# Even part of a fused DFT and feed-forward kernel leaves its bank mid-sum, mixed by unit over VectorE, ScalarE and GpSimd; late last tile; early edge products

## The chip, the cores and the metric

The kernel runs on one core of one Trainium2 chip. The metric is the device time of an execution in microseconds (us). One early execution of the kernel before took 1646 us. A difference under 2% is called "within 2%" in the prediction. Five engines matter: TensorE (PE in the profile; its weight loads are PEld), VectorE (DVE), ScalarE (ACT), GpSimd (POOL) and SyncE (SP), which only issues transfers here.

## The reference

```python
def _attn_ref(x):                       # x: (8, 3008, 256)
    X = np.fft.fft(x, axis=1)
    X = np.fft.fft(X, axis=2)
    return X.real.astype(np.float32)

def _moe_ref(x, w_in, w_out):           # 24064 tokens, 256 -> 2048 -> 256
    h = np.maximum(x @ w_in, 0.0)
    return (h * h @ w_out).astype(np.float32)

def reference(x, moe_w_in, moe_w_out):
    y = _attn_ref(x)
    return _moe_ref(y.reshape(-1, 256), moe_w_in, moe_w_out)
```

## The kernel before

The kernel uses the symmetry of the transform. Folded inputs go through one table product along the sequence and give P (even part) and Q (odd part). The transform along the 256 features is multiplied into the first weights once, at the start: G1 for P and G2 for Q. A token and its mirror then need `relu(E + O)` and `relu(E - O)`, with E = G1'P and O = G2'Q. One row of Q is an exception: it belongs to the even part (the "edge") and must keep its sign in the mirror.

The work is cut into 25 chunks of up to 512 such pairs, and each chunk into units: one unit is 128 of the 2048 hidden features for 512 pairs. An ordinary unit takes three matmuls in one bank of PSUM, the memory that takes up TensorE's sums. E + O is read by ScalarE, then -2 O is added with the third weights G3, and ScalarE reads E - O:

```python
    def x_front(c, u):                                   # [indices shortened]
        xb = psx.tile([P, 512], F32, name="xb", tag="x")
        for sn, G in ((0, G1), (1, G2)):
            mm(xb, G[:, fs], PQ[b][sn][...], sn == 0, sn == 1)
        act(r_s(c, u), xb, AF.Relu)
        return (c, u, xb, None)

    def x_back(cur):                                     # two steps later
        if xb is None: return
        mm(xb, G3[:, fs], PQ[b][1][...], False, True)
        relu_d(c, u, lambda o, i: act(o, xb[:, :, i], AF.Relu))
```

Some units are split: two matmuls into two banks, and the two sums are made outside. That saves a matmul and costs VectorE three operations:

```python
    def x_split(c, u):
        xs = [xo, xe]                                    # two banks
        mm(xo, G2, Q); mm(xe, G1, P)
        act(bs[0], xs[0], AF.Copy, bias=0.0, scale=1.0)
        def add():
            stt(out=bs[1], in0=ebc[c], scalar=gE2[:, u : u + 1], in1=bs[0], op0=ALU.mult, op1=ALU.subtract)
            sat(r_s(c, u), bs[0])                        # relu(xe + bs[0]), VectorE
            relu_d(c, u, lambda o, i: sat(o, bs[1]))     # relu(xe + bs[1]), VectorE

    YZ = [(0, 0)] * 3 + [(2, 0)] * 3 + [(5, 1)] * 9 + [(7, 1)] * 9 + [(0, 0)]   # splits, ScalarE squares per chunk
```

VectorE (in some cases ScalarE) squares the hidden values, and the second layer runs through each chunk while the next one is being made:

```python
        for grp in groups:
            ops += [one(grp, j, fc) for j in range(len(grp)) for fc in range(NFC)]
...
    for c in range(4):                                   # output weights: 32-bit load, VectorE casts them
        nc.gpsimd.dma_start(out=wot[c], in_=moe_w_out[...])
    def wcast(c):
        nc.vector.tensor_copy(wout16[:, cs, :], wot[c])
    spread([(lambda c=c: wcast(c)) for c in range(4)], 3, 7)
    LAG = 2
    SQ = 1                                               # units between a finished unit and its square
```

## Time and profile before

| Measured | Value |
|---|---|
| time, median of 3 (the 1646 us among them) | 631.49 us |
| span of the profiled execution | 628.5 us |
| matmuls | 4682 |
| TensorE / VectorE / ScalarE / GpSimd busy | 96 / 85 / 76 / 11% |

From the page of the kernel before, parts 1 and 2: busy time of each engine (us, share of the span, instructions), and the granted TensorE clock, in tenths, in 40 equal slices of the span.

```profile
PE 606.4 (96%) x4682; PEld 446.9 (71%) x4682; DVE 536.8 (85%) x827; ACT 479.3 (76%) x872; POOL 68.8 (11%) x97
...
PEclk9979999999999999999999999999999999999999
...
```

A busy TensorE need not be at its peak: it counts as busy for 606.4 us, while the ideal spacings below sum to 596.1. So spacing matters more. The chain of waits has dozens of pieces like this one (start, length, what and how many):

```profile
86.01 0.88 PE po L73 x8
```

Eight second-layer matmuls of 256 columns start some 109 ns apart. In this trace the median spacing of each width N from 62 to 512 columns lies within 1.5 ns of N/2.4 + 2.5 ns (256 columns: 109 ns, 512: 217). I call that line the ideal spacing of a matmul of N columns, and whatever the next matmul starts later than that a gap. The 46 pieces of 31 columns lie above the line: they take 28 ns, and are counted at about 27. All ideal spacings sum to 596.1 us, all gaps to 17.3 us; the rest is 10.9 us ahead of the first matmul and 4.0 us after the last.

Where the gaps are is seen in the busy time by stretch (kernel before; stretch, its length, busy time and instructions of PE, PEld, DVE, ACT, POOL, granted clock, DMA share, GB/s):

```profile
24.00:40.00 16.00, 10.80 (x79) 7.33 (x78) 13.71 (x28) 15.30 (x33) 0.00 (x0) 1.00 0.91 190
40.00:48.00 8.00, 6.87 (x36) 4.46 (x35) 4.65 (x11) 2.69 (x6) 0.00 (x0) 0.57 0.04 0
...
450.00:500.00 50.00, 50.00 (x410) 39.26 (x408) 46.61 (x63) 39.43 (x70) 1.08 (x2) 1.00 0.31 49
```

In the first two stretches TensorE is not full, and in the second the clock falls to a mean of 0.57: the trace has it at one half from 40.2 us on for 6.8 us, and second-layer matmuls of 256 columns then start 213 ns apart in place of 109. I call this a half-clock spell. Later (third line) TensorE is full, beside a VectorE at 93% and a ScalarE at 79%. Two groups of waits of TensorE stand behind the start (the kernel before; total us, times, longest):

```profile
PE xb L73 <- ACT h L605: 4.1, 5, 1.8
PE pf L73 <- DVE cosT L279: 2.0, 2, 1.1
...
```

One small loss lies later. The edge products use weights of 3 columns (timeline of the kernel before; start, length, what):

```profile
142.95 0.60 PE L73 MATMUL po<-wout,h 128*128 128x256 f16 x4
143.48 0.64 PE L73 MATMUL pf<-cosT,eall 127*3 127x377 f16 x3
144.06 0.39 PE L73 MATMUL xb<-pt,G 128*128 128x512 f16 x1
```

Four matmuls should take 4 x 109 = 437 ns, yet the next starts 530 ns after the first: some 95 ns extra. The same comes on the way back, and also around the last tile's 16 columns: 18 times in all.

### The profile page before, as it was taken

Reading aid. Unit: us, or ns where it says so; the run is one execution under the profiler, and the core shown is the slowest. Engines: PE = TensorE matmul, PEld = TensorE weight load, DVE = VectorE, ACT = ScalarE, POOL = GpSimd, SP = SyncE. Lnnn points to the kernel's source line nnn. Section 1 sums busy time; section 2 is a strip of 40 time slices with the busy share of each in tenths; the row PEclk is TensorE's granted clock in tenths of the full one; section 3 lists DMA queues with packets and bytes.
Section 4 is the critical chain, followed back from the end, with each engine's and each line's share of the span. In section 5 each row is a group of like instructions: output and inputs, shape, how many; then the busy total and the mean of one; then the engine's idle time right before and its main releaser. Section 6 shows DMA issues by size and latency. Waiting matters only on the chain.

```text
span 628.5 us, 11983 instructions
## 1 busy us (share of the span) xinstructions
PE 606.4 (96%) x4682; PEld 446.9 (71%) x4682; DVE 536.8 (85%) x827; ACT 479.3 (76%) x872; POOL 68.8 (11%) x97
## 2 busy tenths in 40 slices
PE   3969999999999999999999999999999999999997
PEld 1547677776777777777777768777787778877786
DVE  8788799995988989889899879998999899999920
ACT  6768887777788788777887877877877778878871
POOL 8204043120120005000000000000000000000000
PEclk9979999999999999999999999999999999999999
DMA  8944477682591416714313314314233134131112
GB/s 282 300 83 138 120 181 205 156 225 57 91 208 36 59 44 170 138 34 59 43 51 44 57 34 63 43 47 48 54 56 43 51 43 59 52 46 48 52 52 68
DMA packets 37342, 57.21 MB, mean 91 GB/s; under 512 B 7262, under 2 KB 31490, under 8 KB 37286
## 3 DMA queue, kind: packets, MB, share of 16 engines
q0 software_dynamic: 7536, 30.21, 27.9%
q1 hardware_dynamic: 29702, 26.23, 13.4%
q8 instruction: 36, 0.59, 0.4%
q14 instruction: 20, 0.16, 0.1%
q10 hardware_dynamic: 48, 0.02, 0.0%
HBM read 29.02 MB, written 24.64 MB: 85 GB/s over the span
## 4 chain that ended last, share of the span: by engine, by line
PE 92%; DVE 6%; ACT 1%; issue 0%; DVEq 0%; POOL 0%; POOLq 0%; ACTq 0%
PE po L73 52%; PE xb L73 25%; PE pf L73 6%; PE xo L73 4%; PE xe L73 4%; DVE h L663 2%; PE warm L73 1%; DVE u L330 1%; DVE v L342 0%; DVE w L348 0%; DVE wout L723 0%; DVE tm L248 0%; ACT h L605 0%; DVE tm L236 0%; DVE tt L183 0%
## 5 line engine op out<-in xcount | busy, mean ns | idle before, releaser
L73 PE MATMUL po<-wout,h 128*128 128x256 f16 x3024 | 433.6, 273 | 0.0
L73 PEld LDWEIGHTS <-h 128*128 128x128 f16 x3024 | 287.2, 98 | 113.9 <-issue 0.4
L663 DVE TENSOR_TENSOR h<-h 128x2048 f16<-128x2048 f16 (+1 forms) x174 | 207.8, 1195 | 41.1 <-ACT h L651 36.5
L605 ACT ACTIVATE h<-xb 128x512 f16<-128x512 f32 (+1 forms) x270 | 159.2, 590 | 67.8 <-PE xb L73 67.1
L73 PE MATMUL xb<-qt,G 128*128 128x512 f16 (+11 forms) x720 | 203.6, 322 | 4.9 <-ACT h L605 4.1
L651 ACT ACTIVATE h<-xb 128x512 f16<-128x512 f32 (+2 forms) x286 | 160.4, 567 | 20.3 <-PE xb L73 13.9
L73 PEld LDWEIGHTS <-G 128*128 128x128 f16 x1384 | 130.3, 98 | 36.7 <-issue 9.6
L636 DVE CUSTOM_DVE_ANT_0 h<-xe,bs 128x512 f16<-128x512 f32 x228 | 145.9, 680 | 0.0
L73 PE MATMUL xb<-pt,G 128*128 128x512 f16 (+9 forms) x360 | 103.8, 324 | 0.3 <-DVE qt L424 0.2
L632 DVE SCALAR_TENSOR_TENSOR bs<-eb,gE,bs 128x512 f32<-128x512 f16 x114 | 85.0, 745 | 9.1 <-ACT bs L629 8.4
L629 ACT ACTIVATE bs<-xo 128x512 f32<-128x512 f32 x114 | 68.5, 601 | 21.0 <-PE xo L73 16.3
L557 ACT ACTIVATE os<-po 128x512 f32<-128x512 f32 x94 | 56.4, 600 | 19.1 <-PE po L73 16.7
L614 POOL DMA_DIRECT2D eb<-qt x28 | 15.4, 551 | 349.6 <-DVE bs L632 297.1
L73 PE MATMUL xo<-qt,G 128*128 128x512 f16 (+14 forms) x152 | 43.4, 327 | 0.0
L73 PE MATMUL xe<-pt,G 128*128 128x512 f16 (+14 forms) x152 | 43.4, 326 | 0.0
L330 DVE TENSOR_TENSOR u<-x 127x765 f16<-127x765 f32 x32 | 29.7, 945 | 0.0
L101 POOL DMA_INDIRECT x<-in_x_dram,idx x18 | 27.6, 1536 | 5.8 <-issue 4.5
L73 PEld LDWEIGHTS <-w 127*128 127x128 f16 (+1 forms) x192 | 21.6, 118 | 7.2 <-issue 1.4
L73 PE MATMUL pf<-cosT,w 127*128 127x377 f16 (+1 forms) x96 | 20.5, 327 | 2.0 <-DVE cosT L279 2.0
L124 POOL DMA_DIRECT2D x<-in_x_dram x14 | 7.9, 562 | 123.3 <-DVE u L334 122.7
L348 DVE TENSOR_TENSOR w<-v 127x381 f16<-127x381 f16 x64 | 20.7, 352 | 0.0
L73 PE MATMUL pf<-sinT,w 127*127 127x377 f16 (+1 forms) x96 | 20.7, 323 | 0.0
(103 smaller groups left out, 216.9 us busy)
## 6 DMA issues: line engine op xcount, KB each, us to landing
out_dram<-os SPq DMA_DIRECT2D x157, 128.0 KB
x<-in_x_dram POOLq DMA_DIRECT2D x14, 756.0 KB, 9.6
wst<-in_moe_w_in_dram POOLq DMA_DIRECT2D x4, 512.0 KB, 6.9
wot<-in_moe_w_out_dram POOLq DMA_DIRECT2D x4, 512.0 KB, 9.1
eb<-qt POOLq DMA_DIRECT2D x14, 128.0 KB, 6.7
x<-in_x_dram SPq DMA_DIRECT2D x2, 756.0 KB
x<-in_x_dram,idx POOLq DMA_INDIRECT x18, 10.7
gE<-G SPq DMA_DIRECT2D x16, 0.2 KB
```

The lines of the kernel that those rows point to most:

```text
L73: nc.tensor.matmul(o, l, r, start=start, stop=stop, skip_group_check=True)
L101: nc.gpsimd.indirect_dma_start(out=x4[0:NP, 2 + s, q : q + rows, :].rearrange("p q d -> p (q d)"), out_offset=None, in_=bass.AP(tensor=x.t ...
L330: return lambda: vt(u[k, s, q0 : q0 + NQ // 2, 1:D], x4[k, s, q0 : q0 + NQ // 2, 1:D], x4[k, 3 - s, ::-1, :][:, q0 : q0 + NQ // 2, D - 1 : ...
L348: return lambda: vt(w[k, i, q : q + 3, 0 : P - 1], vs[s][k, q : q + 3, 1:P], vs[s][k, q : q + 3, D - 1 : P : -1], op=ALU.add if i < 2 else ...
L557: act(os_, po, AF.Copy, bias=0.0, scale=HS * HS)
L605: act(r_s(c, u), xb, AF.Relu)
L614: nc.gpsimd.dma_start(out=ebc[c][:, o : o + l], in_=PQ[b][1][P - 1 : P, i : i + l].unsqueeze(1).to_broadcast([1, P, l]))
L629: act(bs[0], xs[0], AF.Copy, bias=0.0, scale=1.0)
L632: stt(out=bs[1], in0=ebc[c][:, 0:n], scalar=gE2[:, u : u + 1], in1=bs[0], op0=ALU.mult, op1=ALU.subtract)
L636: nc.vector._custom_dve(TENSOR_ADD_SAT, out=o, in0=xs[1], in1=t, s0=BIG, s1=0.0)
L651: relu_d(c, u, lambda o, i: act(o, xb[:, :, i], AF.Relu))
L663: vt(h2, h2, h2, op=ALU.mult)
```

## The change

The intent is to have fewer matmuls without filling VectorE. A taken unit has one bank and two matmuls. After E alone is in the bank, a copy of 2 E leaves it (VectorE in one operation, or ScalarE with an addition on GpSimd); then O is added in the bank, ScalarE reads relu(E + O), and VectorE reads the mirror as bank plus copy. The signs of G1 and G2 are turned so that this is a plain addition. X puts back the edge row's sign; it is made one step ahead. Which unit takes which way is a table. Other parts: the output weights are cast by their load (256 KB each in place of 512), two small operations go from VectorE to ScalarE, three warm-up matmuls (whose sums nobody reads) go, squares come two units later, the second layer takes a chunk's last tile late, and the edge products and the last tile use 65 weight columns. ScalarE also takes two or three pair squares per chunk where it took one (SQA), and the edge row's loads go from GpSimd's queue to SyncE's.

```diff
+    def edge(c, u):                                    # [cut: memo]
+        X = h2v(c, u)[:, u % 2, n : 2 * n]
+        ts(out=X, in0=ebc[c][:, 0:n], scalar1=gE2[:, u : u + 1], scalar2=None, op0=ALU.mult)
-    def x_split(c, u):                                 # [cut, shown above]
+    def x_take(c, u):
+        mm(xb[:, o : o + l], G1[:, fs], PQ[b][0][:, i : i + l], o == 0, True)
+        X = edge(c, u)
+        if KINDS[c][u] == "q":
+            act(T, xb, AF.Copy, bias=0.0, scale=-2.0)
+            nc.gpsimd.tensor_tensor(T, T, X, op=ALU.add)
+        else:
+            stt(out=T, in0=xb, scalar=-2.0, in1=X, op0=ALU.mult, op1=ALU.add)
     def x_back(cur):
+        if T is not None:
+            mm(xb[:, 0, o : o + l], G2[:, fs], PQ[b][1][:, i : i + l], False, True)
+            act(r_s(c, u), xb, AF.Relu, scale=-1.0)
+            mirrors.append((1, ...TENSOR_ADD_SAT, in0=xb[:, 0, i], in1=T[:, i]...))
+            return
-    YZ = [(0, 0)] * 3 + [(2, 0)] * 3 + [(5, 1)] * 9 + [(7, 1)] * 9 + [(0, 0)]
+    KINDS = ["rrrrrrrrrrrrrrrr"] * 3 + ["rrrrrrrrdrrrrrrr"] * 3 + ["rrrrrrdrrrdrqrdr"] + ["rrdrqrdrrrdrqrdr"] * 8
+        + ["rrrrrrrdqrqdrqdr"] + ["qdqrdqrdqrqdrqdr"] * 8 + ["rrdrdrrdrrdrdrrd"]
+    SQA = [()] * 6 + [(2, 6)] * 9 + [(1, 4, 6)] * 9 + [()]       # pair squares on ScalarE
-            ops += [one(grp, j, fc) for j in range(len(grp)) for fc in range(NFC)]
+            ops += [one(grp, j, fc) for fcs in (range(NFC - 2 * nf), range(NFC - 2 * nf, NFC))
+                    for j in range(len(grp)) for fc in fcs]
-        nc.gpsimd.dma_start(out=wot[c], in_=moe_w_out[...])
+        nc.gpsimd.dma_start(out=wout16[:, c * NFC // 4 : (c + 1) * NFC // 4, :], in_=moe_w_out[...])
-    spread([(lambda c=c: wcast(c)) for c in range(4)], 3, 7)
-                (nb, lambda q: eall[k, blk, q, bs[0] : bs[0] + nb], q, cosT)
+                (MW, lambda q: ewide((blk * NQ + q) * B + bs[0]), q, cosT)      # MW = 65
-    SQ = 1
+    SQ = 3
+        if si + 1 < len(steps) and KINDS[steps[si + 1][0]][steps[si + 1][1]] != "r":
+            edge(*steps[si + 1])
```

In KINDS "r" is an ordinary unit, "d" leaves through VectorE and "q" through ScalarE and GpSimd. The other cut parts turn signs and move small tiles.

More of the change, by code (lines that the diff above doesn't have):

```diff
@@ L131 @@
         nc.sync.dma_start(out=x4[0:NP, s, :, :], in_=up(0, s))
-    jrow = iota("jrow", [P, P], [[1, P]], 1, 0)
+    jm = h2p.tile([P, 3, P], F32, name="jm", tag="h2")
+    jrow = jm[:, 0]
+    nc.gpsimd.iota(jrow, pattern=[[1, P]], base=1, channel_multiplier=0,
+                   allow_small_or_imprecise_dtypes=True)
     idx2 = iota("idx2", [P, 1], [[0, 1]], NQ // 2 * (NP - 1), -NQ // 2, I32)
@@ L135 @@
     wst = [h2p.tile([P, 2, F // 4], F32, name="wst", tag="h2") for _ in range(4)]
-    wot = [h2p.tile([P, NFC // 4, D], F32, name="wot", tag="h2") for _ in range(4)]
     wS = 2.0 * math.pi / S
@@ L191, in dmats @@
         pv = nc.gpsimd
-        t = tgp.tile([P, P], F32, name="td", tag="td")
-        m = tgp.tile([P, P], F32, name="md", tag="md")
+        t, m = jm[:, 1], jm[:, 2]
         pv.tensor_scalar(out=m, in0=jrow, scalar1=pidx[:, 0:1], scalar2=None, op0=ALU.mult)
@@ L207, in hi @@
         def hi():
-            ts(out=csD[:, 1, :, 0:P:2], in0=csD[:, 0, :, 0:P:2], scalar1=-1.0, scalar2=None,
-               op0=ALU.mult)
-            nc.vector.tensor_copy(csD[:, 1, :, 1:P:2], csD[:, 0, :, 1:P:2])
+            act(csD[:, 1, :, 0:P:2], csD[:, 0, :, 0:P:2], AF.Copy, bias=0.0, scale=-1.0)
+            nc.scalar.copy(csD[:, 1, :, 1:P:2], csD[:, 0, :, 1:P:2])
         return fin, hi
@@ L307, in gmat @@
             mm(ps, sinD[:, t, :], win16(c)[:, t, :], t == 0, t == 1)
-        act(G1[:, cs], pc, AF.Copy, bias=0.0, scale=1.0 / HS)
-        act(G2[:, cs], ps, AF.Copy, bias=0.0, scale=-1.0 / HS)
+        act(G1[:, cs], pc, AF.Copy, bias=0.0, scale=-1.0 / HS)
+        act(G2[:, cs], ps, AF.Copy, bias=0.0, scale=1.0 / HS)
     def gneg(c):
@@ L313, in gneg @@
         ts(out=G3[:, cs], in0=G2[:, cs], scalar1=s3[:, 0:1], scalar2=None, op0=ALU.mult)
-    eall = const.tile([P, 2, NQ, B], F16, name="eall")
+    MW = P // 2 + 1
+    eflat = const.tile([P, 2 * NQ * B + MW], F16, name="eall")
+    nc.gpsimd.memset(eflat, 0.0)
+    eall = eflat[:, 0 : 2 * NQ * B].rearrange("p (s q b) -> p s q b", s=2, q=NQ)
     bf = {}
@@ L437, in stage1_ops, with ewide @@
         return ops
+    def ewide(o):
+        return eflat[k, o : o + MW]
     def e_ops(bs):
@@ L481 @@
         g += n
-    YZ = [(0, 0)] * 3 + [(2, 0)] * 3 + [(5, 1)] * 9 + [(7, 1)] * 9 + [(0, 0)]
-    def plan(c, y, z):
-        if chunks[c][1] != CH:
-            return (), ()
-        return ([u for u in range(NFC) if (u * y + 8) % NFC < y],
-                [p for p in range(NFC // 2) if (p * z + 4) % (NFC // 2) < z])
-    PLAN = [plan(c, *YZ[c]) for c in range(len(chunks))]
+    KINDS = ["rrrrrrrrrrrrrrrr"] * 3 + ["rrrrrrrrdrrrrrrr"] * 3 + ["rrrrrrdrrrdrqrdr"] + ["rrdrqrdrrrdrqrdr"] * 8 + ["rrrrrrrdqrqdrqdr"] + ["qdqrdqrdqrqdrqdr"] * 8 + ["rrdrdrrdrrdrdrrd"]
+    SQA = [()] * 6 + [(2, 6)] * 9 + [(1, 4, 6)] * 9 + [()]
     gE = const.tile([P, NFC], F16, name="gE")
@@ L500, in e_double @@
     def e_double():
-        ts(out=gE2, in0=gE, scalar1=2.0, scalar2=None, op0=ALU.mult)
+        ts(out=gE2, in0=gE, scalar1=-2.0, scalar2=None, op0=ALU.mult)
     h2t = {}
@@ L567, in f @@
                 o = n + n % P + t0 if s == 1 else t0
-                w = 2 * m if s == 2 else m
+                w = MW if s == 2 else m
                 mm(st["o"][0:w, j, :], h2v(c, fc // nf)[:, fc % (2 * nf), o : o + w], wout16[:, fc, :],
@@ L604, in x_front @@
                        j == 0 and sn == 0 and o == 0, sn == 1)
-        act(r_s(c, u), xb, AF.Relu)
+        act(r_s(c, u), xb, AF.Relu, scale=-1.0)
         return (c, u, xb, None)
@@ L613, in e_spread @@
         for (b, i, o, l) in segs:
-            nc.gpsimd.dma_start(out=ebc[c][:, o : o + l],
+            nc.sync.dma_start(out=ebc[c][:, o : o + l],
                               in_=PQ[b][1][P - 1 : P, i : i + l].unsqueeze(1).to_broadcast([1, P, l]))
-    nsplit = [0]
-    def x_split(c, u):
-        g0, n, nf, segs = chunks[c]
-        fs = slice(u * P, (u + 1) * P)
-        xs = [psx.tile([P, 512], F32, name=nm, tag="x")[:, 0:n] for nm in ("xo", "xe")]
-        for t, G, sn in ((xs[0], G2, 1), (xs[1], G1, 0)):
-            for (b, i, o, l) in segs:
-                mm(t[:, o : o + l], G[:, fs], PQ[b][sn][:, i : i + l], o == 0, True)
-        nsplit[0] += 1
-        bs = tgp.tile([P, 2, CH], F32, name="bs", tag=("tt", "tm")[nsplit[0] % 2])
-        bs = [bs[:, j, 0:n] for j in range(2)]
-        act(bs[0], xs[0], AF.Copy, bias=0.0, scale=1.0)
-        def add():
-            stt(out=bs[1], in0=ebc[c][:, 0:n], scalar=gE2[:, u : u + 1], in1=bs[0], op0=ALU.mult,
-                op1=ALU.subtract)
-            def sat(o, t):
-                nc.vector._custom_dve(TENSOR_ADD_SAT, out=o, in0=xs[1], in1=t, s0=BIG, s1=0.0)
-            sat(r_s(c, u)[:, 0, :], bs[0])
-            relu_d(c, u, lambda o, i: sat(o[:, 0, :], bs[1]))
-        return (c, u, None, add)
@@ L642, in x_back @@
-    def x_back(cur):
-        c, u, xb = cur[:3]
-        if xb is None:
+    DLAG = {'q': 1, 'd': 1, 'p': 1}
+    mirrors = []
+    taken = [0]
+    tbuf = []
+    made_x = {}
+    def edge(c, u):
+        if (c, u) not in made_x:
+            n = chunks[c][1]
+            X = made_x[c, u] = h2v(c, u)[:, u % 2, n : 2 * n]
+            if KINDS[c][u] == "p":
+                nc.gpsimd.tensor_scalar(out=X, in0=ebc[c][:, 0:n], scalar1=gE2[:, u : u + 1], scalar2=1.0,
+                                        op0=ALU.mult, op1=ALU.mult)
+            else:
+                ts(out=X, in0=ebc[c][:, 0:n], scalar1=gE2[:, u : u + 1], scalar2=None, op0=ALU.mult)
+        return made_x[c, u]
@@ new lines, in x_take @@
+    def x_take(c, u):
+        g0, n, nf, segs = chunks[c]
+        if not tbuf:
+            tbuf.extend(tgp.tile([P, 2, CH], F32, name="bs", tag=t) for t in ("tt", "tm"))
+        i = taken[0]
+        taken[0] += 1
+        T = tbuf[i // 2 % 2][:, i % 2, 0:n]
+        fs = slice(u * P, (u + 1) * P)
+        xb = psx.tile([P, 512], F32, name="xb", tag="x")[:, 0:n]
+        for (b, i, o, l) in segs:
+            mm(xb[:, o : o + l], G1[:, fs], PQ[b][0][:, i : i + l], o == 0, True)
[3 more added lines that the diff above has]
+            nc.gpsimd.tensor_tensor(T, T, X, op=ALU.add)
+        else:
+            stt(out=T, in0=xb, scalar=-2.0, in1=X, op0=ALU.mult, op1=ALU.add)
+        return (c, u, xb.unsqueeze(1), T)
@@ new lines, in x_back @@
+    def x_back(cur):
+        c, u, xb, T = cur
+        g0, n, nf, segs = chunks[c]
+        if T is not None:
+            fs = slice(u * P, (u + 1) * P)
+            for (b, i, o, l) in segs:
+                mm(xb[:, 0, o : o + l], G2[:, fs], PQ[b][1][:, i : i + l], False, True)
+            act(r_s(c, u), xb, AF.Relu, scale=-1.0)
+            mirrors.append((DLAG[KINDS[c][u]], lambda: relu_d(c, u, lambda o, i: nc.vector._custom_dve(
+                TENSOR_ADD_SAT, out=o[:, 0, :], in0=xb[:, 0, i], in1=T[:, i], s0=BIG, s1=0.0))))
@@ L645, in x_back @@
             return
-        g0, n, nf, segs = chunks[c]
         for j in range(nf):
@@ L650, in x_back @@
                 mm(xb[:, j, o : o + l], G3[:, fs], PQ[b][1][:, i : i + l], False, True)
-        relu_d(c, u, lambda o, i: act(o, xb[:, :, i], AF.Relu))
+        relu_d(c, u, lambda o, i: act(o, xb[:, :, i], AF.Relu, scale=-1.0))
     def x_square(cur):
@@ L657, in x_square @@
         h2 = h2v(c, u)
-        if u // 2 in PLAN[c][1]:
+        if u // 2 in SQA[c]:
             nf = chunks[c][2]
@@ L675 @@
         nc.gpsimd.dma_start(
-            out=wot[c], in_=moe_w_out[c * F // 4 : (c + 1) * F // 4, :].rearrange(
+            out=wout16[:, c * NFC // 4 : (c + 1) * NFC // 4, :], in_=moe_w_out[c * F // 4 : (c + 1) * F // 4, :].rearrange(
                 "(c p) o -> p c o", p=P))
@@ L689 @@
     warm = psx.tile([P, 512], F32, name="warm", tag="x")
-    for _ in range(15):
+    for _ in range(13):
         mm(warm, ez[:, 0, 0, :], ez[:, 0, 0:4, :], True, True)
@@ L696 @@
     gmat(0)
-    for _ in range(3):
+    for _ in range(2):
         mm(warm, ez[:, 1, 0, :], ez[:, 1, 0:4, :], True, True)
@@ L719 @@
         side.setdefault(c * (c - 1) // 2, []).extend([lambda c=c: gmat(c), lambda c=c: gneg(c)])
-    def wcast(c):
-        cs = slice(c * NFC // 4, (c + 1) * NFC // 4)
-        nc.vector.tensor_copy(wout16[:, cs, :], wot[c])
-    spread([(lambda c=c: wcast(c)) for c in range(4)], 3, 7)
     spread(rd1[2:], 1, 8)
@@ L740 @@
         for bb, lo, hi in FOLD.get(b, []):
-            spread(sum(fold_ops(bb), []), at(lo), at(hi))
+            ops = sum(fold_ops(bb), [])
+            spread(ops, at(lo), at(hi))
         side.setdefault(at(0.0) + 1, []).append(lambda bb=b + 1: alloc_pq(bb))
@@ L753 @@
     for si, (c, u) in enumerate(steps):
-        if u == 0 and PLAN[c][0]:
-            side.setdefault(si - 3, []).append(lambda c=c: e_spread(c))
+        if u == 0 and KINDS[c].strip("r"):
+            late = any(chunks[c][3][-1][0] == b + 1 != chunks[c][3][0][0] for b in EGRP)
+            side.setdefault(si - (1 if late else 6), []).append(lambda c=c: e_spread(c))
     LAG = 2
-    SQ = 1
+    SQ = 3
     flight = []
@@ L777 @@
         take = [mmq.pop(0) for _ in range(-(-len(mmq) // max(1, due - si)))]
-        flight.append((x_split if u in PLAN[c][0] else x_front)(c, u))
+        flight.append((x_front if KINDS[c][u] == "r" else x_take)(c, u))
         h = len(take) // 2
@@ L784 @@
         posts += [f() for f in take[h:]]
+        due_now = [f for k, f in mirrors if k <= 0]
+        mirrors[:] = [(k - 1, f) for k, f in mirrors if k > 0]
+        for f in due_now:
+            f()
         for p in posts:
@@ L789 @@
             rest.pop()()
+        if si + 1 < len(steps) and KINDS[steps[si + 1][0]][steps[si + 1][1]] != "r":
+            edge(*steps[si + 1])
         if len(made) > SQ:
             retire()
-        if len(flight) > 1 and flight[-2][3]:
-            flight[-2][3]()
         for f in side.get(si, []):
             f()
-    if flight[-1][3]:
-        flight[-1][3]()
     while flight:
@@ L800 @@
         made.append(flight.pop(0))
+        while mirrors:
+            mirrors.pop(0)[1]()
         while made:
```

## The prediction

> **What bounds it.** TensorE. Matmuls run without a gap from 48 to 624.5 us of the 628.5 us span (busy time by stretch), and the chain of waits is 92% TensorE. There each matmul follows as soon as its columns allow: eight second-layer matmuls of 256 columns take 0.87 us (timeline), 109 ns each. [...] With that spacing I estimate all 4682 matmuls at 596 us, the changed program's 4631 at 587 us. The rest is 10.9 us before the first matmul, 14 us lost up to 48 us (cold clock, waits, a 6.8 us half-clock spell near 41-48 us), 3 us lost later, and 4 us for the last store. VectorE is 85% busy, ScalarE 76%, GpSimd 11%.
>
> **What changes.**
> 1. An ordinary unit costs three 512-column matmuls, a split or taken one two. Split before: 114; taken: 155. 41 x 0.216 us, less the shorter pieces: -8.2 us of TensorE, all on the chain. A taken unit also holds one bank, not two.
> 2. Warm-up matmuls 18 to 15: -0.65 us.
> 3. Edge products use 65 weight columns, not 3, the last tile 65, not 16. In the trace each change between 128 columns and 3 or 16 costs some 95 ns extra, 18 times: -1.7 us.
> 4. Start: four casts of the output weights (0.60 us each) and two small operations leave VectorE, squares retire two units later, the second layer takes each chunk's last tile late. TensorE waits 10 us between 24 and 48 us, first for ScalarE (evictions every 0.48 us), then for VectorE (cosine table, squares). I expect 3 us back (0 to 6).
> 5. Load elsewhere, from start-to-start times (ScalarE eviction 0.48, half square 0.95; VectorE square 1.13, take 0.66, saturating add 0.60). Late chunk: eleven taken units, six through ScalarE and GpSimd, three pair squares on ScalarE; TensorE about 23.6 us, ScalarE 21, VectorE 20, GpSimd six additions[...]. ScalarE thus rises from 78% to about 90% there. VectorE falls[...]. I allow 2 us of new TensorE waits.
>
> Sum: 631.5 - 8.2 - 0.65 - 1.7 - 3 + 2, about 620 us.
>
> **Prediction:** 619.5 us, 8 in 10 between 613 and 627. Faster by over 2% (under 618.9): 0.44; within 2%: 0.53; slower: 0.03.
>
> **What would show it.** (1) 4631 matmuls, sum of ideal spacings 9 us lower. (2) First real matmul about 0.5 us earlier. (3) No 95 ns gaps around edge products. (4) Matmul waits between 24 and 48 us shorter; the half-clock spell shorter or gone. (5) In the late half TensorE gapless, ScalarE about 90% busy, VectorE lower than before[...].
>
> **What would make it wrong.** GpSimd additions far longer[...]: then the bank's second reader comes late, TensorE waits for banks in the second half, and the gain halves or goes. ScalarE at 90% may delay the first read of a taken bank, and so its second matmul. If the start stays limited by ScalarE and the clock still falls, item 4 gives nothing (623). If the half-clock spell vanishes and the waits halve, the time is near 615.

Where a cut is marked, something was taken out. 631.5 - 8.2 - 0.65 - 1.7 - 3 + 2 comes to 619.95, about 620 us. The 2 us of new waits are worked out from no measurement. "That spacing" is the ideal spacing as defined above. "Cold clock" is what the trace shows before 16.3 us: the warm-up matmuls of 512 columns start 427 ns apart, later ones 216.

## The result, and the profile after

| | Before | After |
|---|---|---|
| median | 630.98 us (4 runs) | 615.3 us (4 runs) |
| ratio after / before | | 0.9756 (95%: 0.974 to 0.9773) |
| span of the profiled execution | 628.5 us | 613.2 us |

A ratio is the mean time of one kernel's runs over the mean of the other's runs of the same rounds, so it is not quite the ratio of the two medians. Executions over 1.5% slower than the fastest of the same kernel are left out of the means. The changed kernel was run again (control below): 616.14 us, ratio 0.9786 (0.9765 to 0.9808). So the gain is 2.1 to 2.4%. The first comparison is clearly faster by over 2%; the control's interval contains 2%.

The page after, parts 1 and 2:

```profile
PE 592.0 (97%) x4631; PEld 443.1 (72%) x4631; DVE 493.4 (80%) x855; ACT 522.9 (85%) x949; POOL 146.6 (24%) x138
...
PEclk9999999999999999999999999999999999999999
...
```

The same stretches of the changed kernel:

```profile
24.00:40.00 16.00, 11.66 (x85) 7.95 (x83) 13.36 (x31) 16.00 (x36) 0.00 (x0) 1.00 0.85 185
40.00:48.00 8.00, 8.00 (x67) 6.55 (x66) 6.38 (x10) 6.13 (x12) 0.16 (x1) 1.00 0.02 0
...
450.00:500.00 50.00, 50.00 (x396) 38.41 (x394) 46.47 (x75) 46.55 (x83) 18.55 (x13) 1.00 0.30 54
```

In this execution the clock no longer falls at 40 us; in most of the control's executions (below) the mean clock, 0.997, fits a spell of 3.4 us. In the late stretch TensorE stays full, while ScalarE has risen from 79 to 93% and GpSimd from 2 to 37%; VectorE stays at 93%. The waits of TensorE at the start:

```profile
PE xb L73 <- ACT h L606: 3.7, 5, 1.4
...
PE pf L73 <- DVE cosT L279: 0.4, 1, 0.4
...
```

The edge products no longer cost extra (timeline after: two matmuls of 376 columns, then the next one 0.32 us after the first, which is their ideal spacing):

```profile
142.97 0.48 PE L73 MATMUL pf<-cosT,eall 127*65 127x376 f16 x2
143.29 0.38 PE L73 MATMUL xb<-pt,G 128*128 128x512 f16 x1
```

The span divides as follows. All columns are worked out from the traces as described above (us); the gaps are put down by when they begin.

| Kernel | ideal spacings | ahead of first matmul | gaps to 24 us | gaps 24-48 us | gaps after 48 us | after last matmul | span |
|---|---|---|---|---|---|---|---|
| before | 596.1 | 10.9 | 3.5 | 10.6 | 3.1 | 4.0 | 628.5 |
| after | 587.2 | 11.0 | 4.0 | 5.8 | 1.1 | 4.0 | 613.2 |

So of 15.3 us, 8.9 are columns, 4.8 the start and 2.0 the later gaps, less 0.5 for small losses up to 24 us.

### The profile page after: what moved, and what is told of

Same layout as the page of the kernel before. It is cut to its first block, busy times and chain, and to the rows that moved or that the text cites. A ratio compares the mean times of both kernels' runs of the same rounds, so it can differ in the third digit from the quotient of the medians.

```text
span 613.2 us, 12145 instructions
## 1 busy us (share of the span) xinstructions
PE 592.0 (97%) x4631; PEld 443.1 (72%) x4631; DVE 493.4 (80%) x855; ACT 522.9 (85%) x949; POOL 146.6 (24%) x138
## 4 chain that ended last, share of the span: by engine, by line
PE 94%; ACT 2%; DMA 2%; DVE 1%; issue 0%; POOL 0%; DVEq 0%; POOLq 0%; ACTq 0%
PE po L73 54%; PE xb L73 34%; PE pf L73 6%; DMA x<-in_x_dram,idx 2%; ACT h L606 1%; DVE u L333 1%; ACT h L670 1%; ACT cosT L260 0%; ACT G L309 0%; ACT G L308 0%; ACT sinT L264 0%; DVE h L682 0%; DVE v L345 0%; DVE tm L236 0%; DVE qt L426 0%
## 5 line engine op out<-in xcount | busy, mean ns | idle before, releaser
L73 PE MATMUL xb<-qt,G 128*128 128x512 f16 (+16 forms) x824 | 230.9, 321 | 4.5 <-ACT h L606 3.7
L682 DVE TENSOR_TENSOR h<-h 128x2048 f16<-128x2048 f16 (+1 forms) x147 | 176.0, 1201 | 4.6 <-ACT h L670 4.6
L650 POOL TENSOR_TENSOR bs<-bs,h 128x512 f32<-128x512 f32 x68 | 93.5, 1375 | 345.1 <-ACT bs L649 299.8
L606 ACT ACTIVATE h<-xb 128x512 f16<-128x512 f32 (+1 forms) x229 | 139.0, 607 | 28.4 <-PE xb L73 27.7
L670 ACT ACTIVATE h<-xb 128x512 f16<-128x512 f32 (+1 forms) x239 | 139.9, 592 | 26.3 <-PE xb L73 22.1
L73 PE MATMUL xb<-pt,G 128*128 128x512 f16 (+16 forms) x512 | 146.4, 323 | 0.1
L663 DVE CUSTOM_DVE_ANT_0 h<-xb,bs 128x512 f16<-128x512 f32 (+2 forms) x161 | 104.7, 654 | 43.5 <-ACT h L662 43.5
L662 ACT ACTIVATE h<-xb 128x512 f16<-128x512 f32 (+1 forms) x155 | 96.0, 620 | 8.0 <-PE xb L73 6.5
L652 DVE SCALAR_TENSOR_TENSOR bs<-xb,h 128x512 f32<-128x512 f32 (+1 forms) x87 | 58.2, 669 | 21.0 <-PE xb L73 17.9
L633 DVE TENSOR_SCALAR h<-eb,gE 128x512 f16<-128x512 f16 (+1 forms) x155 | 66.6, 431 | 0.5 <-DMA eb<-qt 0.5
L680 ACT ACTIVATE h<-h 128x1024 f16<-128x1024 f16 x45 | 48.7, 1082 | 0.0
L679 ACT ACTIVATE h<-h 128x1024 f16<-128x1024 f16 x45 | 47.8, 1063 | 0.0
L649 ACT ACTIVATE bs<-xb 128x512 f32<-128x512 f32 x68 | 42.8, 630 | 0.5
## 6 DMA issues: line engine op xcount, KB each, us to landing
wout<-in_moe_w_out_dram POOLq DMA_DIRECT2D x4, 256.0 KB, 10.3
```

The source lines that it names most:

```text
L73: nc.tensor.matmul(o, l, r, start=start, stop=stop, skip_group_check=True)
L606: act(r_s(c, u), xb, AF.Relu, scale=-1.0)
L633: ts(out=X, in0=ebc[c][:, 0:n], scalar1=gE2[:, u : u + 1], scalar2=None, op0=ALU.mult)
L650: nc.gpsimd.tensor_tensor(T, T, X, op=ALU.add)
L652: stt(out=T, in0=xb, scalar=-2.0, in1=X, op0=ALU.mult, op1=ALU.add)
L662: act(r_s(c, u), xb, AF.Relu, scale=-1.0)
```

## The experiments

Theory A: TensorE sets the time everywhere, so the gain is its columns (8.9 us), the start (VectorE's four casts made the cosine table late, and the clock fell), and the 95 ns gaps. Rival B: the lighter side engines and freed banks pay. For the start the rival is the late squares and the late last tile. All runs below gave correct results. Ratios are against the kernel before on the same chip.

### Start: the cast alone

```diff
 # kernel before
-    wot = [h2p.tile([P, NFC // 4, D], F32, name="wot", tag="h2") for _ in range(4)]
-            out=wot[c], in_=moe_w_out[...]
+            out=wout16[:, c * NFC // 4 : (c + 1) * NFC // 4, :], in_=moe_w_out[...]
-    spread([(lambda c=c: wcast(c)) for c in range(4)], 3, 7)
```

> The kernel before with one part of the change: the output weights are cast to 16 bits by their load, so four casts leave VectorE's start. Theory A (TensorE is the limit everywhere; the start lost 4.4 us because VectorE was late with the cosine table, and the half-clock spell followed from that): 2.5 to 4.5 us less than before, the half-clock spell gone. Rival B (the gain of the start comes from squares that retire later and from the last tile taken late): within 1 us of before, the spell still there.

Measured: 626.79 us, ratio 0.9941 (0.9922 to 0.9961), 3.7 us less. The gaps between 24 and 48 us fell from 10.6 to 5.7 us, and the stretch that held the spell has the full clock (busy time by stretch of this run):

```profile
40.00:48.00 8.00, 7.20 (x60) 5.85 (x59) 5.23 (x12) 5.96 (x12) 0.00 (x0) 1.00 0.05 2
```

In this execution 1.8 us of it was lost again before 16 us: TensorE waited 2.4 us for the first weights' cast. The casts' removal (by a load that casts) is shown to be enough for the gain of the start. That it worked by way of the cosine table is only argued: TensorE's waits for the table fell from 2.0 to 0.8 us, but those for ScalarE's evictions fell too, from 4.1 to 2.4 us.

### Start: late squares and late last tile alone

```diff
 # kernel before
-            ops += [one(grp, j, fc) for j in range(len(grp)) for fc in range(NFC)]
+            ops += [one(grp, j, fc) for fcs in (range(NFC - 2 * nf), range(NFC - 2 * nf, NFC))
+                    for j in range(len(grp)) for fc in fcs]
-    SQ = 1
+    SQ = 3
```

> The kernel before with only the other part of the start: squares retire two units later and the second layer takes the last tile of each chunk late. Theory A: within 1.5 us of before, the half-clock spell still there or shorter. Rival B: 2.5 to 4.5 us less than before and no spell. Away from the start both expect nothing, since TensorE had no gaps there.

Measured: 629.11 us, ratio 0.9979 (0.9963 to 0.9994), 1.3 us less. The spell was still there, 3.4 us in place of 6.8 in the profiled execution (busy time by stretch of this run):

```profile
40.00:48.00 8.00, 7.12 (x46) 5.14 (x46) 5.09 (x12) 3.95 (x8) 0.00 (x0) 0.79 0.14 19
```

Three of its six executions have a mean clock of 0.993 to 0.995, as the kernel before has. This part matters little by itself.

### Start: all of it, with the old split units

The edit is both of the above, the two small operations on ScalarE, and 13 + 2 warm-up matmuls in place of 15 + 3.

> The kernel before with all of the start's parts (cast by the load, two small operations on ScalarE, three warm-up matmuls fewer, late squares, late last tile), and the old split units. Theory A: 4 to 5.5 us less than before (0.65 of it the warm-up matmuls), no half-clock spell. If the sums of the parts are right, the changed kernel is then 10 to 11 us less than this one: 8.2 of columns, 1.7 of the edge products.

Measured: 626.44 us, ratio 0.9937 (0.992 to 0.9955), 4.0 us less; the span is 623.4 us, 5.1 less. By medians this is 0.35 us less than the cast alone, so beside it the late squares show no gain of their own. The gaps from 24 to 48 us are 5.8 us, just as in the changed kernel. The span of the changed kernel is 10.2 us less than this, as expected of columns and edge products.

### Narrow edge products back

```diff
 # changed kernel
-                (MW, lambda q: ewide((blk * NQ + q) * B + bs[0]), q, cosT)
+                (nb, lambda q: eall[k, blk, q, bs[0] : bs[0] + nb], q, cosT)
-                w = MW if s == 2 else m
+                w = 2 * m if s == 2 else m
```

> The changed kernel with edge products of 3 weight columns and a last tile of 16, as before. Theory A: 18 extra gaps of some 95 ns come back, 1.5 to 1.9 us more than the changed kernel. Rival (the gaps are hidden by slack of the other engines and cost nothing at the end): no difference, under 0.5 us.

Measured: 617.49 us, ratio 0.9811 (0.9786 to 0.9836). The gaps after 48 us rose from 1.1 to 2.8 us, by the 1.7 expected; the span by 1.1 only, since this execution lost 0.7 less at its start. By ratio it is 3.5 us above the first runs of the changed kernel and 1.6 above the control (by medians 2.2 and 1.4). The trace shows the cost, the times agree in direction, and they alone would not settle it. In the kernel before, each of the 18 changes of the weights' columns costs 93 to 98 ns; with 65 columns none costs over 2 ns. Why a change to 3 or 16 columns costs that is not shown.

### Fewer taken units

KINDS has 113 taken units in place of 155, about as many as were split before.

```diff
 # changed kernel, the chunks that differ
-["rrdrqrdrrrdrqrdr"] * 8 + ["rrrrrrrdqrqdrqdr"] + ["qdqrdqrdqrqdrqdr"] * 8
+["rrdrqrdrrrdrqrrr"] * 8 + ["rrrrrrrrqrrdqrdr"] + ["qrrqrdrrqrqrdrqr"] * 8
```

> The changed kernel with 113 taken units in place of 155, so about as many two-matmul units as before (114), all else as changed. Theory A (columns on TensorE decide): the sum of ideal spacings is 9.1 us higher, and the time 8.5 to 9.5 us above the changed kernel. Rival B (what pays is the shorter work on VectorE and the single bank for each taken unit, not the count): less than 4 us above the changed kernel, since every taken unit still has the new form.

Measured: 624.55 us, ratio 0.9906 (0.989 to 0.9922). The difference of the ratios to the changed kernel, 0.0150, is 9.5 us; against the control's ratio it is 7.6 us. In the traces ideal spacings rose by 9.1 us of a span difference of 10.7; a half-clock spell of 3.4 us that fell into this execution makes the rest. The new form without more two-matmul units gains little beyond the start and the edge products, so rival B falls.

### The old form at the new number

The kernel before, splitting all units that the changed kernel takes, except in the last, short chunk (149).

```diff
 # kernel before
-    PLAN = [plan(c, *YZ[c]) for c in range(len(chunks))]
+    PLAN = [([u for u in range(NFC // ch[2]) if KINDS[c][u] != "r" and ch[1] == CH], plan(c, *YZ[c])[1])
+            for c, ch in enumerate(chunks)]
```

> The kernel before with its old split form at the units that the changed kernel takes (all but those of the last, short chunk): 149 in place of 114. TensorE's ideal spacings fall 7.6 us. VectorE has about 1.86 us for each old split unit, so a late chunk with eleven of them has near 30 us of VectorE work against 23.6 us of TensorE. Theory A with VectorE as the next limit: 25 to 60 us slower than before, VectorE full in the second half, TensorE with gaps. Rival (the old form could have had the columns too): 5 to 8 us faster than before.

Measured: 678.68 us, ratio 1.076 (1.0735 to 1.0785). Of its 73.5 us of gaps, 58.9 come after 48 us. Busy time by stretch and TensorE's longest wait of this run:

```profile
450.00:500.00 50.00, 41.24 (x326) 30.92 (x324) 49.86 (x72) 26.75 (x47) 1.08 (x2) 1.00 0.24 41
```

```profile
PE xe L73 <- DVE h L637: 23.3, 36, 1.2
...
```

VectorE is full (49.86 of 50 us) and TensorE waits for it to release a split unit's bank. So here fewer columns help only if VectorE can keep up, and in the old form it cannot. One thing differs besides the form: this run leaves all 174 pair squares of before on VectorE, the changed kernel 147, two fewer in each late chunk. Those would be 2.4 us per late chunk (2 x 1.2). The gaps after 400 us, 54 us in nine late chunks, are 6 us per chunk. So I estimate that the squares would have closed under half of them; no run tests it.

### All taken units through VectorE

KINDS with every "q" turned into "d".

> The changed kernel with all taken units through VectorE, none through ScalarE and GpSimd. A late chunk gets 6 x 0.66 us more on VectorE, which was 93% busy there, and 6 x 0.48 us less on ScalarE. If the mix by unit is needed: 8 to 25 us slower than the changed kernel, TensorE waiting in the second half for VectorE. If GpSimd's additions only cost VectorE time by holding it up (rival): no slower than 2 us[...].

Measured: 621.29 us, ratio 0.986 (0.9841 to 0.9878), 6.6 us above the changed kernel by ratio (4.7 by the control's). The direction was right and the size expected was too large. Gaps after 48 us are 6.4 us in place of 1.1, and the whole rise lies before the second matmul of a taken unit. (A half-clock spell of 3.4 us also fell into the profiled execution, at 38 us.) What the additions hold up on VectorE is seen in the changed kernel: the 47 edge products that one overlaps took 635 ns on average, the 102 full-size others 345. Without them VectorE is at 98%:

```profile
500.00:550.00 50.00, 49.28 (x398) 38.44 (x397) 48.75 (x84) 40.05 (x66) 0.00 (x0) 1.00 0.27 51
```

### One taken unit more in each of eight early chunks

```diff
 # changed kernel
-["rrdrqrdrrrdrqrdr"] * 8
+["rrdrqrdrdrdrqrdr"] * 8
```

> The changed kernel with one taken unit more (through VectorE) in each of chunks 7 to 14, where VectorE was some 77% and ScalarE 86% busy. TensorE's ideal spacings fall 1.7 us. Theory A: 1.5 to 1.9 us less than the changed kernel. Rival (these chunks are already limited by another engine in order): no gain.

Measured: 613.93 us, ratio 0.9745 (0.9723 to 0.9768). Ideal spacings fell by 1.7 us and the gaps after 48 us stayed at 1.1, but a half-clock spell of 3.4 us lay in the profiled execution, though the start is the same program. The times alone do not tell this from the changed kernel; the trace shows the columns gone and nothing lost for it.

### Control

> The changed kernel itself, unaltered, as a control on the same chip as the next three: some 0.976 of the time of before (615 us), with gaps before 48 us of 9.5 to 12 us, depending on whether a half-clock spell of 3.4 us falls near 37 to 41 us in an execution (it did in three variants whose start is the same).

Measured: 616.14 us (615.5 to 618.09), ratio 0.9786. The profiled execution has no spell, gaps before 48 us of 10.3 us and a span of 613.7 us. The 95% interval leaves "faster by 2%" unclear. Four of its five executions have a mean granted clock of 0.997 and took 615.85 to 618.09 us, the fifth has 1.0 and took 615.5. In the first runs, three with 0.999 or 1.0 took 614.95 to 615.65, and one with 0.997 took 616.31.

### Edge products in their own step

```diff
 # changed kernel
-        if si + 1 < len(steps) and KINDS[steps[si + 1][0]][steps[si + 1][1]] != "r":
-            edge(*steps[si + 1])
```

> The changed kernel with the edge products made in their own step, in place of one step ahead. Theory A (TensorE alone sets the time while the other engines keep up): within 1.5 us of the changed kernel, TensorE still without gaps after 60 us. Rival (the early product is what lets the bank be read in time): gaps in the second half, more than 3 us slower.

Measured: 622.92 us, ratio 0.9888 (0.9869 to 0.9908), 6.4 us above the control of the same call. My expectation failed and the rival held. Gaps after 48 us are 8.9 us in place of 1.1, and the whole rise lies before the second matmul of a taken unit, in which TensorE waits for VectorE to read the bank. That wait is absent in the changed kernel:

```profile
PE xb L73 <- DVE bs L652: 3.8, 11, 0.5
...
```

The busy time by stretch of this run and of the changed kernel, in that order:

```profile
500.00:550.00 50.00, 48.67 (x395) 38.25 (x394) 48.87 (x71) 45.55 (x80) 17.98 (x13) 1.00 0.26 49
```

```profile
500.00:550.00 50.00, 50.00 (x414) 40.10 (x412) 46.65 (x74) 48.34 (x85) 18.18 (x14) 1.00 0.32 55
```

VectorE is at 98% for 93%, and TensorE no longer full. With the product made in its own step, VectorE gets to the bank later, and TensorE waits (the 3.8 us above, 11 times). Two causes are mixed here: the product now stands directly ahead of the read of the bank, and it also takes longer. All edge products (this run, then the changed kernel):

```profile
L633 DVE TENSOR_SCALAR h<-eb,gE 128x512 f16<-128x512 f16 (+1 forms) x155 | 78.7, 508 | 0.0
```

```profile
L633 DVE TENSOR_SCALAR h<-eb,gE 128x512 f16<-128x512 f16 (+1 forms) x155 | 66.6, 431 | 0.5 <-DMA eb<-qt 0.5
```

Those that a GpSimd addition overlaps take 919 ns on average (45 of them), against 635 in the changed kernel. No run separates the two causes.

### Four evictions of the start on VectorE

```diff
 # changed kernel
-        act(G2[:, cs], ps, AF.Copy, bias=0.0, scale=1.0 / HS)
+        ts(out=G2[:, cs], in0=ps, scalar1=1.0 / HS, scalar2=None, op0=ALU.mult)
```

> The changed kernel with four of the eight 512-column evictions of the first weights moved from ScalarE (0.48 us each) to VectorE, which waits there. Theory A (what is left of the start's gaps is ScalarE, evicting at 0.48 us a piece from 22 to 38 us): the gaps between 24 and 40 us, 5.8 us in the changed kernel, fall by 1.2 to 2 us, and the time by 1 to 2.5 us. If VectorE's cosine table is still the limit there: no gain.

Measured: 615.28 us, ratio 0.9762 (0.974 to 0.9783), 1.5 us below the control by ratio, with overlapping intervals. The profiled execution had two half-clock spells, at 19 and at 39 us, and its gaps from 24 to 40 us were 5.5 us against 5.8. The expected fall of 1.2 to 2 us isn't there. ScalarE's load fell from 16.00 to 13.90 us of that stretch and VectorE's rose from 13.36 to 14.90, so ScalarE's evictions alone are not what is left. The spells blur this reading; the next run has the same edit and no spell, and its gaps there are 5.2 us, still only 0.6 less. What limits the rest of the start stays open.

### More taken units

The eviction edit of the last run, and 176 taken units.

```diff
 # changed kernel, chunks 3 to 14
-["rrrrrrrrdrrrrrrr"] * 3 + ["rrrrrrdrrrdrqrdr"] + ["rrdrqrdrrrdrqrdr"] * 8
+["rrrrrrrrdrrrrrrr", "rrrrdrrrdrrrrrrr", "rrdrrrdrrrdrrrdr", "rrrrrrdrdrdrqrdr"] + ["drdrqrdrdrdrqrdr"] * 8
```

> The last one, and 176 taken units in place of 155, the new ones through VectorE in chunks 4, 5 and 7 to 14. TensorE's ideal spacings fall 4.5 us against the changed kernel. Theory A, while VectorE stays under some 95% there: 4 to 6.5 us faster than the changed kernel, near 610 us, no gaps after 60 us. If VectorE fills: gaps between 100 and 380 us, and less than 2 us gained.

Measured: 610.29 us, ratio 0.9689 (0.9668 to 0.971), 6.1 us below the control by ratio: it beats both kernels. Ideal spacings fell by 4.5 us, to 582.7. Gaps after 48 us are 1.5 us. The runs lie on both sides of the 95% in the expectation: at 93% (changed kernel, 450 to 500 us) TensorE was full, at 98% (all through VectorE, 500 to 550 us) it was not. The other 1.6 us of the 6.1 are as large as the last run's difference from the control, whose intervals overlap. VectorE rose from 76 to 88% between 100 and 200 us, and TensorE stayed full (this run, then the changed kernel):

```profile
100.00:200.00 100.00, 100.00 (x770) 72.76 (x769) 88.19 (x152) 77.57 (x140) 13.20 (x15) 1.00 0.59 130
```

```profile
100.00:200.00 100.00, 100.00 (x766) 72.25 (x764) 75.96 (x127) 81.17 (x146) 15.07 (x16) 1.00 0.60 130
```

## Why the prediction was right or wrong

The time, 615.3 us, lies inside the range of 613 to 627, 4.2 us below the middle. The likelier class, within 2%, was missed by a little, and the control alone would have left it unclear. About 1 us of the 4.2 lies in the start value: 631.5 was a median with the 1646 us execution in it.

1. Columns: right. Ideal spacings fell by 8.9 us, as predicted with the warm-up matmuls, and fewer or more taken units moved them and the span alike. The three warm-up matmuls gave less than their 0.65 us: the first real matmul started at 16.57 us, before at 16.83, as it waited 0.9 us for ScalarE's cast of the weights. The old form at the same units lost 48 us, which the prediction did not ask.
2. Edge products: right. The gaps of 95 ns are gone; with narrow weights they come back as 1.7 us.
3. Start: right direction, the term mis-sized, 4.8 us between 24 and 48 us for the predicted 3. Most of it is the half-clock stretch, and part of that is luck: the profiled execution had no spell, while four of the control's five have a mean clock that fits one of 3.4 us (0.997; by my estimate 3.4 us at one half take 0.003 off the mean of a span of 614). The parts: gaps from 40 to 48 us fell from 4.0 us to 0, those from 24 to 40 us only from 6.6 to 5.8. The shorter waits I had counted on were the smaller part. The casts' removal alone did it; the late squares gave 1.3 us alone and nothing visible beside it. What brings a spell is not shown. In the kernel before no gap in the 16 us ahead of the 6.8 us spell was longer than 1.9 us; the gaps from 24 to 40 us sum to 6.6 us. In the changed kernel they sum to 5.8, the longest 1.5, and its profiled execution has no spell, while three runs with the same program at the start have one of 3.4 us.
4. "I allow 2 us of new TensorE waits" failed: there were none, as the gaps after 48 us fell from 3.1 to 1.1 us, of which 1.7 are the edge gaps of item 2. This (2.3 us), the start (1.8) and the start value (1) make up the 4.2 us, less the 0.5 lost up to 24 us and the 0.5 between the sum (620) and the forecast (619.5).
5. Load elsewhere: ScalarE went to 93% in the late half for the predicted 90%. "VectorE falls" holds for the whole (85 to 80%) but not for the late half (93% before and after). Nor did it fall by the new form: the 155 taken units take VectorE 58.2 + 66.6 + 104.7 = 229.5 us, the 114 split ones took 85.0 + 145.9 = 230.9. What fell is the squares, 27 of which went to ScalarE (before, then after):

```profile
L663 DVE TENSOR_TENSOR h<-h 128x2048 f16<-128x2048 f16 (+1 forms) x174 | 207.8, 1195 | 41.1 <-ACT h L651 36.5
```

```profile
L682 DVE TENSOR_TENSOR h<-h 128x2048 f16<-128x2048 f16 (+1 forms) x147 | 176.0, 1201 | 4.6 <-ACT h L670 4.6
```

   So the new form bought 41 more two-matmul units for the same VectorE time. My 20 us for a late chunk were too low. One reason is shown: an edge product takes 345 ns alone (102 of them) and 635 ns where a GpSimd addition overlaps it (47, up to 1144). The trace shows the timing, not the cause. One case (timeline after): the product ends 0.16 us after the addition, in place of 0.34 us after its own start.

```profile
508.08 1.28 POOL L650 TENSOR_TENSOR bs<-bs,h 128x512 f32<-128x512 f32 x1 [1.30 <-ACT bs L649]
...
508.87 0.65 DVE L633 TENSOR_SCALAR h<-eb,gE 128x512 f16<-128x512 f16 x1
```

   GpSimd's 68 additions took 1.38 us on average. But the 36 that no VectorE square overlaps took 1.16 us. The 30 that began while a square ran took 1.64 us on average, and 29 of them ended 1.01 to 1.02 us after that square, whenever they had begun. So they seem to have waited for its end. The squares did not suffer if they began first: those 30 took 1218 ns on average, as much as the ones that no addition overlaps (1216), while the two that began during an addition took 2179 and 2183. One case (timeline after):

```profile
442.55 1.22 DVE L682 TENSOR_TENSOR h<-h 128x2048 f16<-128x2048 f16 x1
...
443.05 1.73 POOL L650 TENSOR_TENSOR bs<-bs,h 128x512 f32<-128x512 f32 x1 [3.57 <-ACT bs L649]
```

6. Not seen: that the early edge products are what keeps the second matmul of a taken unit from waiting. Without them 6.4 us of the gain are lost, perhaps in part because the products then take longer where a GpSimd addition overlaps them (919 ns for 635). The prediction named the danger (the first read of a taken bank may come late), but for ScalarE; the run shows it for VectorE.

## What to carry to other kernels

Where TensorE has no gaps, count its columns first, and then ask which form of the side work lets more of them go: here nearly the same units (149 of 155) in the older form, with fewer squares on ScalarE, cost 48 us. An engine at 93% can be harmless, but then the order of its queue decides: a product moved one step ahead was worth 6.4 us. Look at the granted clock at the start, since the kernel before lost time there twice: 6.6 us of gaps from 24 to 40 us, and then 4.0 us, most of them in a half-clock spell. And before you call an engine slow, split its operations by what runs beside them: GpSimd's mean of 1.38 us was 1.16 us free and 1.64 us behind a square.
